# Softcap attention and two gated MLPs on one core: attention on four planner threads, first pairs by block rows, slots shared otherwise

## The chip, the core and the metric

The program runs on one core of a Trainium2 chip. A core has five engines with queues of their own: TensorE (matmuls and their weight loads), VectorE (DVE), ScalarE (ACT), GpSimd (POOL) and SyncE (SP), which here starts the DMAs. They run beside each other and wait for each other through semaphores. The metric is the device time of one execution in microseconds (us); lower is better.

## What is computed

Attention with softcapped scores for 4 batches and 12 heads of 448 tokens and 64 columns; its output, 1792 tokens by 768, goes through a gated MLP (768 to 1536 to 768, sigmoid gate) and then through a second one (768 to 2048 to 768) whose activation is h cos(h). The weights arrive as 64-bit floats.

```python
scores = scale * np.matmul(q, k.transpose(0, 1, 3, 2))
scores = cap * np.tanh(scores / cap)
scores = scores - np.max(scores, axis=-1, keepdims=True)
attn = np.exp(scores)
attn = attn / (np.sum(attn, axis=-1, keepdims=True) + 1e-09)
x = np.matmul(attn, v)           # then (batch, token, head * 64)
gate = 1.0 / (1.0 + np.exp(-(x @ w_gate)))
x = gate * (x @ w_val) @ w_out
h = x @ w_in
out = (h * np.cos(h)) @ w_out2
```

## The kernel before

**Arithmetic.** Every matmul operand is split into a high and a low part that TensorE takes at its fast rate, and a product is three matmuls: high by high, high by low, low by high (`mm3`, `mm3s`). The names in the trace follow this: `wh`, `wl` are a weight tile's parts, `xh`, `xl` or the two halves of `x` those of the activations, `gh`, `gl` those of the gated product, `zh`, `zl` those of the hidden layer of the second MLP. The high part is a cast on ScalarE, the low part a subtraction on VectorE or GpSimd (`high`, `low`, `block_split`). A weight is converted from 64-bit words first (`convert`: two operations on ScalarE, L420 and L421, four on VectorE, L424, L432, L440 and L448); the result is kept in DRAM for later use (`kept`). Weights of the second MLP are converted in the background (`bg`, tiles `bf`, `braw`).

**Stages.** The tokens go in two halves of 896 (two batches each). Attention runs over 24 pairs of heads, batch by batch; pair i has transposes of q and k (L1329, split into `qs` and `ks` on VectorE, L1336 and L1340), four score products (L1363), tanh (L1374) and exp (L1394) on ScalarE, sums on GpSimd (L1406) and VectorE (L1417, "softmax total"), the product with the values (L1434), the sum over partitions (L1453), a reciprocal (L1467) and a product with it. For the first 12 pairs the result is split into `xh` and `xl`, for the last 12 it is kept as `x1r`. Then follow, for the first half, the gate and value products (`gate_value_plain`, stage A of half 0: 24 tiles of 6 steps of 6 matmuls) and the output product (`result`, stage B). For the second half the gate and value products, and for both halves the first product of the second MLP, are made in pairs of weight tiles: `pair_products` makes seven products of half the size in place of eight (numbers 1 to 7, made in the order 1, 2, 6, 5, 7, 4, 3, each over three blocks j of the contraction, 63 matmuls in all). It takes sums of blocks of the activations (`block_sums`, tiles `x`, `t`, `yr`, `y`, `x1r`) and of the weights (`sums`), and `pair_sums` evicts the seven products from their banks (L816, L825). The whole order is: attention; A and B of half 0; A (first pair products) and B of half 1; the cosine stage of half 1, then of half 0, each with eight pair products C, whose results go through the chain `hidden` (u, n, u, sine, u = h times cosine, zh, zl), and four output groups D (`out_group`), in the order C C C D C C D C C C D D.

**What sets the order.** Nothing is ordered by hand. Generators ("threads") yield operations, and `Order.run` takes the operation that could start first by a table of durations, plus a penalty of its thread; the engines' queues then hold the operations in that order. Threads wait on conditions: a free slot of 49 half-size tiles (`mids`, `get`, `get_w` with a range of weight tiles per stage, W_A0 to W_CD), one of five big tiles (`bigs`), a bank of PSUM, or a word in `done`. Attention is one thread with penalty 0, so its operations enter the queues in the order in which they are written, on whatever engine they run. `whole`, which issues all other TensorE work, has penalty 4 us until attention ends, the weights' threads 0.3 (W_PEN). First weights are loaded from pair 18 on (W_FROM), and until attention ends three are converted at most (LEAD).

## Time and profile before

| | us |
|---|---|
| median of 3 runs | 1239.87 (1237.41 to 1241.43) |
| the profiled execution | 1238.03 |
| its span, first to last instruction | 1236.2 |
| TensorE busy (matmuls) | 1177.0 (95%) |
| VectorE busy | 929.1 (75%) |
| ScalarE busy | 672.1 (54%) |
| GpSimd busy | 252.4 (20%) |
| mean granted TensorE clock | 0.983 |

In the profile, PE is TensorE, DVE VectorE, ACT ScalarE, POOL GpSimd. L708 and L720 are the lines of all matmuls of the plain and of the pair products, L1226 that of the output groups. TensorE's matmuls overlap, so its busy time is a union; time per matmul is read from a long stretch without waits. A wait is the idle time of an engine before an instruction, with the instruction that ended it. By time: attention ends near 247 us, A and B of half 0 near 406 and 495, A and B of half 1 near 661 and 755; the cosine stage of half 1 ends near 999, that of half 0 at 1232.

### The profile page before, as it was taken

What the parts mean: (1) busy time and instruction counts of PE and PEld (TensorE: products, weight loads), DVE (VectorE), ACT (ScalarE), POOL (GpSimd) and SP (SyncE); (2) the same over time, 40 slices, a digit from 0 to 9 for tenths busy, and PEclk for the clock granted to TensorE, in tenths of its full rate; (3) what the DMA queues carried; (4) which work ended last, traced back from release to release, by engine and by line L of the source; (5) the groups of instructions that cost most, each with busy time, mean ns of one, the idle gap of its engine ahead of it and who ended that gap; (6) DMA issues with size and microseconds to landing.
All of it is one profiled execution on the core that took longest, in us unless ns stands there. A gap on an engine that the chain in (4) does not pass through costs nothing.

```text
span 1236.2 us, 15864 instructions
## 1 busy us (share of the span) xinstructions
PE 1177.0 (95%) x6090; PEld 995.7 (81%) x6090; DVE 929.1 (75%) x1128; ACT 672.1 (54%) x785; POOL 252.4 (20%) x139
## 2 busy tenths in 40 slices
PE   8999978999999999999998998889999998999998
PEld 4444545599999999888887996789999997989898
DVE  6999886689887966888889645865678878275862
ACT  6888876756555644444446433665347347361730
POOL 3666543400011000223321000111122212011200
PEclk9999998999999999999998998899999998999999
DMA  7432233177876575334433730112106322121203
GB/s 181 109 79 68 71 85 91 57 256 229 276 258 204 186 253 183 130 128 141 159 111 121 260 141 17 56 44 77 39 26 205 90 77 77 38 66 39 77 1 90
DMA packets 126187, 148.16 MB, mean 120 GB/s; under 512 B 49952, under 2 KB 98976, under 8 KB 126112
## 3 DMA queue, kind: packets, MB, share of 16 engines
q1 hardware_dynamic: 125824, 147.09, 38.4%
q8 instruction: 48, 0.79, 0.3%
q14 instruction: 27, 0.22, 0.1%
q10 hardware_dynamic: 288, 0.07, 0.0%
HBM read 112.13 MB, written 35.00 MB: 119 GB/s over the span
## 4 chain that ended last, share of the span: by engine, by line
PE 70%; DVE 7%; ACT 2%; issue 2%; DVEq 0%; ACTq 0%
PE pt L708 28%; PE pt L720 23%; PE pt L1226 18%; DVE wl L494 1%; DVE zl L1167 1%; ACT wh L483 1%; DVE h L816 1%; DVE val L816 1%; DVE x L1052 1%; DVE sg L893 1%; DVE e L648 1%; ACT x L1046 0%; PE pt L1434 0%; DVE part L816 0%; DVE u L1150 0%
## 5 line engine op out<-in xcount | busy, mean ns | idle before, releaser
L720 PE MATMUL pt<-x,wh 128*128 128x448 f32 x1260 | 349.4, 373 | 10.5 <-DVE x L1052 4.3
L720 PEld LDWEIGHTS pt<-x,wh 128*128 128x128 f32 x1260 | 239.1, 190 | 40.1 <-ACT x L1046 7.2
L494 POOL TENSOR_TENSOR wl<-f,wh 128x768 fp32r<-128x768 f32 x53 | 101.8, 1922 | 442.3 <-ACT wh L483 403.3
L720 PE MATMUL pt<-x,wl 128*128 128x448 f32 x504 | 188.3, 374 | 3.7 <-DVE wl L494 2.9
L483 ACT CAST wh<-f 128x768 fp32r<-128x768 f32 (+1 forms) x164 | 123.3, 777 | 83.6 <-DVE f L648 47.8
L1226 PE MATMUL pt<-wh,zh 128*128 128x384 f32 x448 | 151.1, 337 | 9.2 <-ACT zh L1164 9.2
L1226 PE MATMUL pt<-wh,zl 128*128 128x384 f32 x448 | 151.2, 337 | 4.4 <-DVE zl L1167 4.4
L1226 PE MATMUL pt<-wl,zh 128*128 128x384 f32 x448 | 150.4, 336 | 0.0
L1374 ACT ACTIVATE p<-pt,tanh_scale 112x896 f32<-112x896 f32 x96 | 92.0, 1009 | 46.1 <-PE pt L1363 46.1
L720 PEld LDWEIGHTS pt<-x,wl 128*128 128x128 f32 x504 | 95.9, 190 | 17.3 <-DVE wl L494 8.6
L494 DVE TENSOR_TENSOR wl<-f,wh 128x768 fp32r<-128x768 f32 x83 | 82.3, 996 | 21.2 <-ACT wh L483 20.9
L1249 DVE TENSOR_TENSOR acc<-pt,acc 128x384 f32<-128x384 f32 x84 | 46.7, 556 | 63.2 <-PE pt L1226 62.5
L1226 PEld LDWEIGHTS pt<-wh,zh 128*128 128x128 f32 x448 | 84.8, 189 | 10.6 <-ACT zh L1164 10.5
L1226 PEld LDWEIGHTS pt<-wh,zl 128*128 128x128 f32 x448 | 84.6, 189 | 6.5 <-DVE zl L1167 6.5
L708 PE MATMUL pt<-gl,wh 128*128 128x448 f32 x288 | 83.5, 372 | 3.7 <-DVE gl L937 3.7
L1434 PE MATMUL pt<-p,v 112*64 112x448 f32 x384 | 77.5, 545 | 9.6 <-ACT p L1374 9.6
L1394 ACT ACTIVATE p<-p,cap_sb 112x1792 f32<-112x1792 f32 x48 | 86.2, 1797 | 0.0
L708 PE MATMUL pt<-xh,wh 128*128 128x448 f32 x288 | 85.4, 378 | 0.0
L1363 PEld LDWEIGHTS pt<-qs,ks 64*112 64x112 f32 x576 | 47.0, 173 | 47.2 <-ACT p L1374 21.2
L1226 PEld LDWEIGHTS pt<-wl,zh 128*128 128x128 f32 x448 | 84.8, 189 | 0.1
L708 PE MATMUL pt<-xl,wh 128*128 128x448 f32 x288 | 84.5, 375 | 0.0
L708 PE MATMUL pt<-xh,wl 128*128 128x448 f32 x288 | 84.3, 374 | 0.0
(115 smaller groups left out, 2075.9 us busy)
## 6 DMA issues: line engine op xcount, KB each, us to landing
f<-kept SPq DMA_DIRECT2D x100, 384.0 KB, 3.4
kept<-f SPq DMA_DIRECT2D x36, 384.0 KB, 3.2
braw<-in_moe_w_in_dram SPq DMA_DIRECT2D x16, 768.0 KB, 6.7
kept<-bf SPq DMA_DIRECT2D x32, 384.0 KB, 2.8
braw<-in_moe_w_out_dram SPq DMA_DIRECT2D x16, 768.0 KB, 6.4
raw<-in_moe_w_gate_dram SPq DMA_DIRECT2D x12, 768.0 KB, 5.7
raw<-in_moe_w_val_dram SPq DMA_DIRECT2D x12, 768.0 KB, 5.2
raw<-in_moe_w_out_dram SPq DMA_DIRECT2D x12, 768.0 KB, 5.6
```

The costliest lines, as they stand in the source:

```text
L483: yield act(n, lambda: nc.scalar.copy(out=at(h, 0, n), in_=at(src, o, n)), sc, [h.cell("h")])
L494: lambda e: e.tensor_tensor(out=w.part(1, 0, n), in0=at(src, o, n), in1=w.part(0, 0, n).bitcast(F32), op=ALU.subtract),
L648: lambda: nc.vector.tensor_tensor(out=at(dst, d0, HW), in0=at(x, x0, HW), in1=at(y, y0, HW), op=op),
L708: nc.tensor.matmul(b.ap[:, c, s0:s1], lhsT=w.part(wi, kk * P, P), rhs=x.part(xi, c * S + s0, s1 - s0), start=(first and (wi, xi) == (0, 0) ...
L720: nc.tensor.matmul(b.ap[:, c, s0:s1], lhsT=w.part(wi, o, P), rhs=x[xi][:, s0:s1], start=(first and (wi, xi) == (0, 0)), stop=(last and (wi ...
L816: lambda: nc.vector.tensor_tensor(out=out, in0=src, in1=part, op=ALU.add),
L1226: nc.tensor.matmul(b.ap[:, 0, :NB], lhsT=at(z[zi], t * P, P), rhs=w.part(wi, k * NB, NB), start=(first and (zi, wi) == (0, 0)), stop=(last ...
L1249: lambda: nc.vector.tensor_tensor(out=o, in0=ps(b, 0, NB), in1=o, op=ALU.add),
L1363: nc.tensor.matmul(ps(b, h)[:CP], lhsT=at(ks, ki * S + c * CP, CP)[r], rhs=at(qs, qi * S, S)[r], start=(n_ == 0), stop=(n_ == 2),)
L1374: lambda: nc.scalar.activation(out=two(at(p, 2 * j * S, 2 * S))[:CP], in_=both(b)[:CP], func=AF.Tanh, scale=tanh_scale[:CP],),
L1394: lambda: nc.scalar.activation(out=pv, in_=pv, func=AF.Exp, scale=cap_sb[:CP]),
L1434: nc.tensor.matmul(ps(b)[h * D : (h + 1) * D], lhsT=tv[:CP, h, c, :], rhs=at(p, (2 * j + h) * S, S)[:CP], start=(c == 0), stop=(c == NC - 1),)
```

## The change

Attention becomes four threads, one for each of TensorE, ScalarE, GpSimd and VectorE (`on_pe`, `on_act`, `on_pool`, `on_dve`); what one makes for another is handed over in a dictionary, so each engine's attention work keeps its own order, and other work can be placed between on one engine without the others. The planner subtracts a tenth of the time that an operation has been ready from its penalty (AGE). `whole` has penalty 1 during attention instead of 4 (A_PEN), first weights are loaded from pair 12, and the limit of three converted ones is lifted. The first pair product of each stage that makes pairs goes block row by block row: for each j all seven products, instead of each product over all j (`by_rows`); seven banks are held until the end. `block_sums` finishes all seven blocks of one j before the next j. Slots: wider or shifted weight ranges in stage A of half 1 and in the last stages, two weight pairs loaded ahead instead of three (F_AHEAD), g tiles and the hidden chain's u and n may take a big slot, an attention tile p is freed by its last two readers, and the second half's pair weights are loaded from the last tile of B of half 0 on.

```diff
 class Order:
     LAT = 0.12
+    AGE = 0.1
...
-                pen = th.pen() if callable(th.pen) else th.pen
+                if th.since is None:
+                    th.since = t
+                pen = (th.pen() if callable(th.pen) else th.pen) - self.AGE * (t - th.since)
...
-    LEAD, AHEAD = 3, 4
+    F_AHEAD = 2
+    H_PEN, S_PEN = 0.4, 0.0
+    LEAD, AHEAD = 99, 4
...
-    W_PEN, W_FROM = 0.3, 18
+    W_PEN, W_FROM = 0.3, 12
+    ATT_PEN, A_PEN = 0.0, 1.0
...
-    W_A0, W_B0, W_A1, W_B1, W_CD = (7, 14), (7, 14), (9, 15), (8, 14), (10, 14)
+    W_A0, W_B0, W_A1, W_B1, W_CD = (7, 14), (7, 14), (14, 18), (8, 14), (12, 16)
...
-            yield lambda: len(loaded) < 3
+            yield lambda: len(loaded) < F_AHEAD
...
+        for js in [[j] for j in range(KH)] if by_rows else [range(KH)]:
+            for i in (1, 2, 6, 5, 7, 4, 3):
+                if js[0] == 0:
+                    if i in (1, 3):
+                        at_bank[i] = ((yield from bank()), 0)
...
+                yield from product(i, *at_bank[i], g, X, js, last_use)
+                if js[-1] == KH - 1:
+                    ready.add(i)
...
-                return hf == 1 and "converted" in done and ("B", 0) in done and bigs.left > 0
+                return hf == 1 and ("B", 0) in done and bigs.left > (0 if "converted" in done else BG_RAW)
...
-            yield from pair_products(("pair", "g", p), X, False, GateSink(p))
+            yield from pair_products(("pair", "g", p), X, False, GateSink(p), p == 0)
...
+            if n == KD - 1 and hf == 0:
+                done.add("again")
...
             yield from direct(j, 2)
-        for j in range(KH):
             yield from first_sums(j)
-            yield from later(j, 6)
-        for i in (5, 7, 4, 3):
-            for j in range(KH):
-                yield from direct(j, i) if i == 3 else later(j, i)
+            for i in (6, 5, 7, 4):
+                yield from later(j, i)
+            yield from direct(j, 3)
...
-        u, r = mids.alloc("u", F32), mids.alloc("n", F32)
+        zh = None
+        if in_big():
+            u = bigs.alloc("u", F32)
+            u.refs = 2
+            r, ro = u, n
+            zh = mids.alloc("zh", F32R)
+        else:
+            u, r, ro = mids.alloc("u", F32), mids.alloc("n", F32), 0
...
-            yield from pair_products(("pair", "i", i), X, last, HiddenSink(hf, i))
+            yield from pair_products(("pair", "i", i), X, last, HiddenSink(hf, i), i == 0)
...
+        for gen, name in ((on_pe, "PE"), (on_act, "ACT"), (on_pool, "POOL"), (on_dve, "DVE")):
+            spawn(gen(), ATT_PEN, f"attention {name}")
...
-        spawn(whole(), lambda: 0.0 if "att" in done else 4.0, "PE")
+        spawn(whole(), lambda: 0.0 if "att" in done else A_PEN, "PE")
```

The changed kernel's line numbers differ: L1395 is the score product, L1374 the transposes, L1420 the values product, L1441 the sum over partitions, L715 a plain step, L1575 and L1579 the split of q and k, L1614 the reciprocal, L1623 the product with it, L1593 the softmax total, L431, L439, L447 and L455 the conversion, L501 a weight's low part, L1065 and L1079 a block's low part and a block sum, L827 an eviction, L655 a weight sum, L904 value by gate, L948 gl.

On TensorE, the 17th pair of heads in the kernel before, one values product to the next:

```order
L1434 MATMUL pt<-p_1370,v_1305 64x448 x4
L1434 MATMUL pt<-p_1408,v_1305 64x448 x4
L1363 MATMUL pt<-qs_1316,ks_1348 112x448 x6
L1363 MATMUL pt<-qs_1388,ks_1420 112x448 x6
L1329 MATMUL pt<-ident,qk_1443 128x112 x4
L1453 MATMUL pt<-sum_1417,ones 64x448 x2
L1363 MATMUL pt<-qs_1388,ks_1420 112x448 x12
L1329 MATMUL pt<-ident,qk_1446 128x112 x4
```

And the first pair that holds steps in the changed kernel, pair 15:

```order
L1420 MATMUL pt<-p_1271,v_1156 64x448 x4
L1395 MATMUL pt<-qs_1196,ks_1249 112x448 x6
L715 MATMUL pt<-xh_422,wh_1294 128x448 x2
L715 MATMUL pt<-xl_423,wh_1294 128x448 x2
L715 MATMUL pt<-xh_422,wl_1324 128x448 x2
L1395 MATMUL pt<-qs_1262,ks_1331 112x448 x6
L1374 MATMUL pt<-ident,qk_1303 128x112 x4
L1441 MATMUL pt<-sum_1292,ones 64x448 x2
L1395 MATMUL pt<-qs_1262,ks_1331 112x448 x12
L715 MATMUL pt<-xh_503,wh_1294 128x448 x2
L715 MATMUL pt<-xl_504,wh_1294 128x448 x2
L715 MATMUL pt<-xh_503,wl_1324 128x448 x2
```

The plain steps now begin at pair 15, three of them ahead of its values product, where the kernel before begins with pair 18; ahead of the last values product stand 20 steps, before 16.

On VectorE, attention with the first weight conversion, in the kernel before:

```order
L1467 RECIPROCAL r_1544<-pt 128x448
L1480 TENSOR_TENSOR x1r_1546<-pt,r_1544 128x448
L424 TENSOR_SCALAR f_1517<-f_1517 128x768
L432 TENSOR_SCALAR f_1517<-f_1517 128x768
L440 SCALAR_TENSOR_TENSOR f_1517<-raw_1516,f_1517 128x768
L448 SCALAR_TENSOR_TENSOR f_1517<-f_1517,raw_1516 128x768
L1417 SCALAR_TENSOR_TENSOR sum_1489<-sum_1489,guard,p_1480 112x896
L1336 CAST ks_1580<-pt 128x448
L1340 TENSOR_TENSOR ks_1580<-pt,ks_1580 128x448
```

And a conversion in the changed kernel:

```order
L431 TENSOR_SCALAR f_1454<-f_1454 128x768
L439 TENSOR_SCALAR f_1454<-f_1454 128x768
L447 SCALAR_TENSOR_TENSOR f_1454<-raw_1453,f_1454 128x768
L1575 CAST qs_1577<-pt 128x448
L1579 TENSOR_TENSOR qs_1577<-pt,qs_1577 128x448
L1614 RECIPROCAL r_1614<-pt 128x448
L1623 TENSOR_TENSOR x1r_1615<-pt,r_1614 128x448
L455 SCALAR_TENSOR_TENSOR f_1454<-f_1454,raw_1453 128x768
L1593 SCALAR_TENSOR_TENSOR sum_1550<-sum_1550,guard,p_1541 112x896
L1575 CAST ks_1655<-pt 128x448
```

The conversion's four operations, in one piece ahead of the softmax total before, stand in two places of the pair now; the first conversion (pairs 11 to 14) stands in four.

On VectorE, the end of the second half's value products and the start of its output product, in the kernel before:

```order
L893 TENSOR_TENSOR sg_5188<-val_5310,sg_5188 128x896
L816 TENSOR_TENSOR val_5260<-pt,part_5215 128x448
L893 TENSOR_TENSOR sg_5138<-val_5260,sg_5138 128x896
L937 TENSOR_TENSOR gl_5217<-sg_4074,gh_5216 128x896
L937 TENSOR_TENSOR gl_5332<-sg_4120,gh_5331 128x896
L937 TENSOR_TENSOR gl_5342<-sg_4288,gh_5341 128x896
L937 TENSOR_TENSOR gl_5352<-sg_4333,gh_5351 128x896
```

And in the changed kernel, where two g tiles have been split above these rows:

```order
L827 TENSOR_TENSOR val_5248<-pt,part_5214 128x448
L904 TENSOR_TENSOR sg_5182<-val_5301,sg_5182 128x896
L904 TENSOR_TENSOR sg_5139<-val_5248,sg_5139 128x896
L501 TENSOR_TENSOR wl_5313<-f_5280,wh_5297 128x768
L439 TENSOR_SCALAR bf_5218<-bf_5218 128x768
L948 TENSOR_TENSOR gl_5273<-sg_4321,gh_5272 128x896
L447 SCALAR_TENSOR_TENSOR bf_5218<-braw_5005,bf_5218 128x768
L948 TENSOR_TENSOR gl_5338<-sg_4365,gh_5337 128x896
L455 SCALAR_TENSOR_TENSOR bf_5218<-bf_5218,braw_5005 128x768
L948 TENSOR_TENSOR gl_5349<-sg_4526,gh_5348 128x896
```

Before, all twelve gl stand in one run (one weight's low part among them); now a background conversion's operation stands between one gl and the next.

On VectorE, the start of the cosine stage, the blocks of j = 2 in the changed kernel (y_5904 and y_6026 are the last two output tiles):

```order
L1065 TENSOR_TENSOR x_6074<-t_6057,x_6074 128x448
L1065 TENSOR_TENSOR x_6082<-t_6057,x_6082 128x448
L1079 TENSOR_TENSOR y_5904<-y_6026,y_5904 128x448
L1079 TENSOR_TENSOR y_6026<-y_6026,t_6057 128x448
L655 TENSOR_TENSOR f_5760<-f_5760,e_6025 128x384
L1065 TENSOR_TENSOR x_6096<-y_5904,x_6096 128x448
L501 TENSOR_TENSOR wl_6109<-f_5808,wh_6107 128x768
L827 TENSOR_TENSOR h_6117<-pt,part_6100 128x896
L827 TENSOR_TENSOR part_6100<-pt,h_6117 128x896
L655 TENSOR_TENSOR e_6133<-f_5981 128x384
L1065 TENSOR_TENSOR x_6103<-y_6026,x_6103 128x448
L1065 TENSOR_TENSOR x_6135<-y_6026,x_6135 128x448
```

In the kernel before the blocks of all three j stand in this place, product by product, and of the evictions only the first stands among them; now the blocks of j = 0 and 1 stand higher up, and the last two of j = 2 (products 4 and 3) stand behind the first two evictions of the same pair product.

## Rows read from the trace of the kernel before

**Rows 1.** stages of the span; columns are length, then each engine's busy time, clock, DMA

```profile
163.00:243.20 80.20, 70.25 (x368) 41.95 (x368) 57.00 (x48) 56.82 (x51) 33.23 (x16) 0.91 0.32 87
...
243.20:405.90 162.70, 162.70 (x790) 145.57 (x790) 136.03 (x166) 93.58 (x108) 11.55 (x6) 1.00 0.74 242
...
495.20:660.60 165.40, 159.76 (x758) 140.56 (x757) 140.95 (x178) 80.54 (x109) 45.21 (x24) 1.00 0.42 137
...
660.60:754.90 94.30, 90.58 (x434) 83.42 (x433) 56.93 (x73) 36.58 (x45) 0.00 (x0) 0.96 0.46 155
...
754.90:811.30 56.40, 47.82 (x191) 39.13 (x190) 47.61 (x61) 34.99 (x49) 10.00 (x6) 0.88 0.16 50
...
811.30:844.20 32.90, 29.72 (x170) 29.08 (x169) 14.46 (x17) 16.20 (x25) 0.64 (x1) 1.00 0.06 15
...
1038.20:1075.60 37.40, 31.63 (x170) 30.80 (x169) 15.30 (x18) 17.02 (x26) 0.00 (x0) 0.91 0.05 14
```

**Rows 2.** what TensorE waited for over the span: total, times, longest

```profile
PE pt L1434 <- ACT p L1374: 9.6, 13, 2.4
...
PE pt L1226 <- ACT zh L1164: 9.2, 4, 5.4
...
PE pt L1226 <- DVE zl L1167: 4.4, 6, 1.7
...
PE pt L720 <- DVE x L1052: 4.3, 7, 2.8
...
PE pt L708 <- DVE gl L937: 3.7, 1, 3.7
```

**Rows 3.** TensorE's timeline, values products of five pairs: start, length, what they are

```profile
111.49 3.23 PE L1434 MATMUL pt<-p,v 112*64 112x448 f32 x16 [0.59 <-ACT p L1374]
...
144.56 3.23 PE L1434 MATMUL pt<-p,v 112*64 112x448 f32 x16
...
152.50 3.23 PE L1434 MATMUL pt<-p,v 112*64 112x448 f32 x16
...
162.90 3.23 PE L1434 MATMUL pt<-p,v 112*64 112x448 f32 x16 [2.40 <-ACT p L1374]
...
243.16 2.10 PE L1434 MATMUL pt<-p,v 112*64 112x448 f32 x10
```

**Rows 4.** same view as rows 1, of a head pair each

```profile
111.49:120.09 8.60, 8.01 (x52) 3.99 (x52) 8.19 (x9) 7.06 (x7) 5.34 (x4) 1.00 0.32 79
144.56:152.50 7.94, 7.94 (x54) 4.00 (x53) 6.97 (x8) 7.06 (x7) 4.21 (x3) 1.00 0.31 99
162.90:179.83 16.93, 12.60 (x64) 7.29 (x65) 16.48 (x15) 12.39 (x11) 7.71 (x4) 0.90 0.41 110
```

**Rows 5.** VectorE's softmax totals, min/median/max ns; its conversion operations, busy and mean ns

```profile
L1417 DVE SCALAR_TENSOR_TENSOR sum<-sum,guard,p x24: 1140/1142/4787, 21.1 to 240.2; 112x896 f32<-112x896 f32 x24
...
L440 DVE SCALAR_TENSOR_TENSOR f<-raw,f 128x768 int32<-128x768 int32 x36 | 34.5, 957 | 1.1
...
L432 DVE TENSOR_SCALAR f<-f 128x768 int32<-128x768 int32 x36 | 21.8, 606 | 1.2
```

**Rows 6.** VectorE's gl group, 661 to 684: times, busy and mean ns

```profile
L937 DVE TENSOR_TENSOR gl<-sg,gh 128x896 fp32r<-128x896 f32 x12 | 12.2, 1083 | 0.0
```

**Rows 7.** the start of the cosine stage: a window before it, two VectorE groups, ScalarE

```profile
720.00:755.00 35.00, 35.00 (x175) 32.43 (x174) 10.26 (x16) 7.36 (x11) 0.00 (x0) 1.00 0.15 50
...
L816 DVE TENSOR_TENSOR h<-pt,part 128x896 f32<-128x896 f32 x6 | 6.5, 1091 | 2.2 <-PE pt L720 2.1
...
L1052 DVE TENSOR_TENSOR x<-t,x 128x448 fp32r<-128x448 f32 x5 | 3.0, 620 | 0.7 <-ACT x L1046 0.6
...
754.97 0.91 ACT L1026 COPY y<-pt 128x896 f32<-128x896 f32 x1 [11.73 <-PE pt L708]
```

**Rows 8.** the second output group's start, 1036 to 1052: TensorE, then VectorE

```profile
1044.71 0.69 PE L1226 MATMUL pt<-wh,zh 128*128 128x384 f32 x1 [5.41 <-ACT zh L1164]
...
1041.93 2.09 DVE L1161 TENSOR_TENSOR u<-h,u 128x896 f32<-128x896 f32 x2
```

393 lines of the change are left out of this document (228 added, 165 removed).

## Prediction

> **What bounds the kernel now.** I read the stages first, then who waits on TensorE, then the two engines it waits for. The stages [rows 1]: between 243.2 and 405.9 us TensorE is busy for all 162.7 us, 790 matmuls at 0.206 us each. That is the price of a matmul at full clock, and every stage is held against it: 6 matmuls (one step of a gate or value tile) are 1.24 us, 63 (one pair product) 13.0, 21 (one block row of a pair product) 4.3, 3 (one block of one product) 0.62. A page of the profile puts TensorE at 95% busy, so what can be won is its waits and the stretches at the lower of its two clock levels (1.2 of 2.4 GHz). By stage [rows 1]:
>
> - Attention's end, 163 to 243.2: 70.25 us busy of 80.2, mean clock 0.91.
> - First pair products, 495.2 to 660.6: 756 matmuls should take 155.7 us and take 165.4; 9.7 lost.
> - The second half's first output, 660.6 to 754.9: 432 matmuls, 89.0 against 94.3; 5.3 lost, clock 0.96.
> - The first three cosine pairs, 754.9 to 811.3: 189 matmuls, 38.9 against 56.4; 17.5 lost, clock 0.88.
> - First output group of either half (811.3 and 1038.2): 32.9 and 37.4 us for the same 168 matmuls.
>
> Who is waited for [rows 2]: ScalarE's exp in attention (9.6 us), the zh and zl of the output groups (9.2 and 4.4), the split blocks x (4.3 from VectorE alone) and the first gl (3.7, one wait). [...] So the sum goes stage by stage: which wait goes, and what is late next.
>
> **Attention's second half.** A quiet pair of heads takes 7.94 us, and TensorE is busy for all of it (VectorE 6.97, ScalarE 7.06); while the first half's x is also split, the pair takes 8.60 and VectorE (8.19) is the slowest [rows 4]. In the order, pairs 0 to 10 stand on all engines as before, so they cost the same. From pair 12 on (values product at 111.49) to the last one at 243.16 the kernel before takes 131.7 us [rows 3]. TensorE's own work in it is 12 x 7.94 + 16 steps x 1.24 - 1.6 (the last pairs transpose nothing) = 113.5: 18.2 lost. Where: quiet pairs lose nothing (144.56 to 152.50), the first pair with a weight conversion 2.5 (152.50 to 162.90), the next 16.93 - 10.4 = 6.5, with VectorE 16.48 of 16.93 busy [rows 3, 4]. A conversion's four operations (0.6, 0.6, 0.96 and about 1 us [rows 5]) stand there in one piece between reciprocal and softmax total, and the total, the cast of ks and the next scores stand behind them.
>
> After, 20 steps stand before the last values product, conversions begin at pair 11, and of their four operations one to three stand in a place. Per pair that is 10.4 to 11.7 us on TensorE from pair 15 on, against about 6.97 + 2.2 = 9.2 on VectorE. Where no step stands yet (11 to 14) the conversion's 1.0 to 1.2 us show: VectorE 9.2 to 9.4 where the pair took 8.6; that costs some 2 us. Further waits I put at 7.5 us, 0.8 a pair from 15 on: the pieces are half as long as before, and the steps lie between. So 9.5 lost instead of 18.2: **-8.7**. Bounds: 3 (the pairs without a step alone), which is -15, and 22 (every pair with a piece loses 2.5, as the first did), which is +4. The four steps brought forward are counted by the difference in loss; after attention nothing waits before 495 us [rows 1], so a step earlier is a step saved there.
>
> **First pair products.** The background conversions on VectorE fall from 41 operations to 22 in this stage (counted in the orders), and up to three more weight slots may be held (14 to 18, was 9 to 15), so the waits for weights should fall from 9.7 us to about 2.7. But the first pair now goes block by block. Its last block row starts 8.6 us into the stage; its fourth and third products need blocks that VectorE makes behind two evictions, which themselves wait for products of that same row: by the order the second eviction (5 and 7 done at 11.7, 1.09 each [rows 7]) ends at 12.9 and six operations of 0.5 to 1 us follow to the last block, 16.8. TensorE waits 4 us. Together **-3.0** (-7 to +3; half of either term).
>
> **Second half's first output.** A big slot may now take a g tile before the conversions are done; two of twelve g tiles are split early. But from the third on, conversion operations stand between the gl (the order below). From TensorE's end of the pair products: eviction 0.7, two products with sg to 2.8, a weight's wl 3.7 (768 columns, 0.96 [rows 5]), conversion 4.3, third gl 5.3, and then one gl per 1.02 us [rows 6] plus 0.6 to 0.96 of conversion, to the twelfth at 21.2. Twelve steps alone would end at 14.8; with the last gl they end near 22: 7.2 lost where 5.3 were: **+1.9** (-2 to +4).
>
> **The cosine stage.** Before, block sums go product by product over all three j, so most blocks wait for the last output tile; VectorE does most of them behind it, while from 720 to 755 it was busy for 10.26 us of 35 [rows 7]. After, j = 0 and j = 1 are finished in that idle time and TensorE has two block rows, 8.6 us, before it needs j = 2. ScalarE's copy of the last tile ends at 0.9 [rows 7]; the first three blocks of j = 2 are ready at 3.4, 4.0 and 6.8 (0.62 us an operation [rows 7]), the block of product 7 at 9.0, all before their turn. Products 4 and 3 again stand behind two evictions and one more operation: 12.9 + 0.6 + 0.6 = 14.1 against a turn at 11.7, 2.2 us of waiting. The pair ends at 15.2, the third at 41.2. What is late next is the hidden chain of the second pair: its product u on VectorE stands behind the third pair's evictions (39.4), so the two zl of the first output step come at 46.3 and 47.3, about 4.5 us late. Before, the stage lost 17.5 and the group start 2.9 (the 32.9 us against 30.0, which is 168 at the rate of its undisturbed part); after, 2.2 + 4.5: **-13.7** (-9 to -17).
>
> **Second half of it.** Its blocks were ready in time before, so block rows win nothing and put the first pair's evictions up to 1.7 us later. At its first output group TensorE waited 5.41 us for zh, with u and zl following it on VectorE [rows 8], and the 37.4 us at clock 0.91 hold another 3.4 of the lower clock [rows 1]; by the same reckoning as above the wait is now about 4.1. **-2.5** (-6 to 0). The other group starts: about 1 us less for two of them, **-0.8** (-3 to +1).
>
> **At nothing.** Earlier loads of the pair weights ("again" one tile sooner): the stage's DMA share is at most 0.74 [rows 1]. Seven banks held by a first pair: the eighth takes the next pair's first product, and the two-bank eviction is out 3.1 us after the last row began, before the second asks. Aging in the planner works through the orders counted above. For what I did not count, the 250 us from 243 to 495 that lose nothing now and can only lose, I add **+2** (0 to +4).
>
> Sum: -8.7 - 3.0 + 1.9 - 13.7 - 2.5 - 0.8 + 2 = -24.8. The profiled execution took 1238.03 us (1236.2 span and 1.8 around it), so 1213.2; the median of the runs shown is 1.84 above it: **1215 us**.
>
> **Rivals.**
> 1. The cosine start wins, attention does not. VectorE is already at 6.97 of 7.94 in a quiet pair [rows 4], and a softmax total took up to 4.79 us instead of 1.14 [rows 5]. If the loss in attention stays at 18 and the block rows in the first pair products cost what they save, 11.7 is missing: 1227. Against: steps stand where VectorE was waited for.
> 2. Everything fits better. The waits I walked are taken in turn, with no overlap; of the 34 us I left as waits (9.5, 6.7, 7.2, 6.7, 4.1), a third gone gives 1204, half 1198.
> 3. Slower: VectorE held up by GpSimd. In a pair of heads GpSimd is busy 4.21 us of 7.94 [rows 4] with sums from SBUF, and the conversion pieces now stand in the same pairs. The long total lost 4.79 - 1.14 = 3.65 us [rows 5]. VectorE has 98 us of work in pairs 12 to 23 (the order's operations by the durations above) against the 128 I allow; with 1.3 such holds in every one of twelve pairs it needs 155 and nothing is won; with 1.6 it needs 168, and the kernel takes 1255. Against: one total of 24 is that long before [rows 5], with three conversions in the stretch. The Trainium skill bears on this: "SBUF — State Buffer", section "SBUF: two separate sides", has the second port pair as an exclusive lock, held for a whole instruction, between GpSimd and a VectorE operation with two SBUF inputs; the last two operations of a conversion are of that kind. The longest total agrees with such a lock, its median of 1142 ns shows that it is rarely met; by the rule alone each piece would wait for half of GpSimd's 4.21 us per 7.94, some 0.55 us on average, inside my 0.8.
> 4. It does not do what it says. Attention held 16 steps before and holds 20 now, so little is interleaved that was not; if only that moved, 1235.
>
> **How the numbers follow.** Chances: forecast (1206 to 1224) 0.54; rival 1 (1224 to 1232) 0.18; rival 2 (below 1206) 0.18; rival 4 and other mixtures between 1232 and 1244 0.06; rival 3 0.04. The range reaches from rival 2's end to rival 1's upper side, 1198 to 1232, and leaves out the slower cases and a fifth of rival 2. About 0.3% (3.7 us) is what a measurement of this kernel tells from no change. Faster 0.91, same 0.04, slower 0.05.
>
> **What would show it.** In the profile after: values products 12 to 23 apart by 10 to 12 us and the last near 234 to 240; two to four long waits for x at the first pair of the stages near 485 and 745, each under 3 us; gl waits of 0.3 to 0.8 us in a row behind the pair products; three cosine pairs in about 41 us where 56.4 stood; first output groups waiting 4 to 5 us for zl. It is wrong if attention's end does not move, if totals or conversions on VectorE are often over 2 us, or if weights (wh, wl) are waited for at the block rows.

## The result, and the profile after

The changed kernel takes **1195.54 us** in the median (1195.09 to 1199.94, 4 runs) where the kernel before takes 1239.12 (1237.41 to 1241.43, 4 runs, on the same chip): ratio 0.9655, 95% interval 0.9627 to 0.9683. Forecast were 1215 us and a range of 1198 to 1232. The sign was right; the time lies 2.5 us below the range and the gain is 43.6 us where 24 were forecast.

Stretches of the changed kernel, in the columns of [rows 1] (length; TensorE, its weight loads, VectorE, ScalarE, GpSimd busy; clock; DMA):

```profile
108.91:232.12 123.21, 118.76 (x703) 65.46 (x702) 111.73 (x101) 103.50 (x92) 63.43 (x31) 1.00 0.35 93
...
387.40:475.00 87.60, 87.60 (x434) 81.19 (x433) 69.58 (x99) 47.35 (x61) 1.79 (x1) 1.00 0.67 225
474.90:638.40 163.50, 158.52 (x758) 143.44 (x757) 127.49 (x167) 72.17 (x100) 36.22 (x20) 0.98 0.36 119
638.40:732.70 94.30, 90.19 (x434) 80.34 (x433) 71.41 (x100) 44.69 (x58) 0.00 (x0) 1.00 0.49 163
732.70:773.50 40.80, 38.65 (x191) 35.41 (x190) 31.76 (x40) 28.96 (x39) 12.69 (x7) 1.00 0.28 88
773.50:808.80 35.30, 31.22 (x170) 30.58 (x169) 14.62 (x18) 16.87 (x27) 0.00 (x0) 0.95 0.04 12
1000.90:1036.90 36.00, 32.33 (x170) 31.50 (x169) 14.70 (x18) 16.94 (x27) 0.00 (x0) 0.91 0.04 12
```

The first line is attention from the values product that stands at 111.49 in [rows 3] to the last one. The three cosine pairs take 40.8 us where [rows 1] has 56.4. What TensorE still waits for (total, times, longest), against [rows 2]:

```profile
PE pt L1255 <- ACT zh L1193: 6.1, 2, 3.1
PE pt L1420 <- ACT p L1486: 4.2, 7, 0.6
PE pt L715 <- DVE gl L948: 4.1, 6, 2.2
PE pt L727 <- DVE x L1065: 3.7, 2, 2.2
PE pt L727 <- ACT x L1059: 3.4, 1, 3.4
```

Stage by stage, from the end of TensorE's last matmul of one stage to that of the next in its timeline (us):

| stage | before | changed | difference | forecast |
|---|---|---|---|---|
| attention to the values product of [rows 3], first row | 111.49 | 108.91 | -2.6 | 0 |
| from there to the last values product | 131.7 | 123.2 | -8.5, and 4 steps more inside: -13.4 | -8.7 |
| rest of the first half's gate and value tiles, those 4 steps counted here | 162.9 | 160.3 | -2.6 | +2 (with the next) |
| first half's output | 89.3 | 87.6 | -1.7 | |
| first pair products | 165.4 | 163.4 | -2.0 | -3.0 |
| second half's first output | 94.2 | 94.3 | +0.1 | +1.9 |
| three cosine pairs and first output group | 89.3 | 76.1 | -13.2 | -13.7 |
| second half of the cosine stage, first output group | 37.45 | 35.9 | -1.6 | -2.5 |
| the four other output groups | 181.1 | 176.0 | -5.2 | -0.8 |
| sum | | | -42.2 | -24.8 |

The sum is the difference of the spans, 1236.2 and 1194.0. So 17.4 us were missed, in four places: attention (4.7 and 2.6), TensorE's own pace behind it (6.3), the other output groups (4.4). The rest is within 2 us each.

### The profile page after: what moved, and what is told of

Same layout as the page of the kernel before. It is cut to its first block, busy times and chain, and to the rows that moved or that the text cites. A ratio compares the mean times of both kernels' runs of the same rounds, so it can differ in the third digit from the quotient of the medians.

```text
span 1194.0 us, 15877 instructions
## 1 busy us (share of the span) xinstructions
PE 1159.2 (97%) x6090; PEld 989.7 (83%) x6090; DVE 913.1 (76%) x1127; ACT 668.6 (56%) x785; POOL 258.6 (22%) x140
## 4 chain that ended last, share of the span: by engine, by line
PE 88%; DVE 7%; ACT 2%; issue 1%; SPq 0%; DMA 0%; DVEq 0%; ACTq 0%
PE pt L727 30%; PE pt L715 28%; PE pt L1255 19%; PE pt L1420 5%; PE pt L1395 4%; DVE r L1614 1%; ACT p L1486 1%; PE pt L1374 1%; PE pt L1441 1%; ACT p L1503 1%; DVE sum L1593 1%; DVE gl L948 1%; DVE zl L1196 1%; DVE h L827 0%; SPq L1329 0%
## 5 line engine op out<-in xcount | busy, mean ns | idle before, releaser
L727 PE MATMUL pt<-x,wh 128*128 128x448 f32 x1260 | 344.6, 369 | 7.1 <-DVE x L1065 3.7
L727 PE MATMUL pt<-x,wl 128*128 128x448 f32 x504 | 185.7, 368 | 0.0
L501 POOL TENSOR_TENSOR wl<-f,wh 128x768 fp32r<-128x768 f32 x41 | 80.1, 1957 | 381.8 <-ACT wh L490 297.3
L501 DVE TENSOR_TENSOR wl<-f,wh 128x768 fp32r<-128x768 f32 x95 | 96.8, 1024 | 45.9 <-ACT wh L490 45.6
L715 PE MATMUL pt<-gl,wh 128*128 128x448 f32 x276 | 79.4, 369 | 4.1 <-DVE gl L948 4.1
L715 PE MATMUL pt<-xh,wh 128*128 128x448 f32 x288 | 83.4, 371 | 0.0
L715 PE MATMUL pt<-xl,wh 128*128 128x448 f32 x288 | 81.8, 365 | 0.0
L715 PE MATMUL pt<-xh,wl 128*128 128x448 f32 x288 | 81.8, 365 | 0.0
L1420 PE MATMUL pt<-p,v 112*64 112x448 f32 x384 | 77.5, 545 | 4.2 <-ACT p L1486 4.2
L1395 PEld LDWEIGHTS pt<-qs,ks 64*112 64x112 f32 x576 | 46.2, 171 | 41.9 <-ACT p L1486 16.7
```

The lines of the kernel that those rows point to most:

```text
L501: lambda e: e.tensor_tensor(out=w.part(1, 0, n), in0=at(src, o, n), in1=w.part(0, 0, n).bitcast(F32), op=ALU.subtract),
L715: nc.tensor.matmul(b.ap[:, c, s0:s1], lhsT=w.part(wi, kk * P, P), rhs=x.part(xi, c * S + s0, s1 - s0), start=(first and (wi, xi) == (0, 0) ...
L727: nc.tensor.matmul(b.ap[:, c, s0:s1], lhsT=w.part(wi, o, P), rhs=x[xi][:, s0:s1], start=(first and (wi, xi) == (0, 0)), stop=(last and (wi ...
L1395: nc.tensor.matmul(ps(b, h)[:CP], lhsT=at(ks, ki * S + c * CP, CP)[r], rhs=at(qs, qi * S, S)[r], start=(n_ == 0), stop=(n_ == 2),)
L1420: nc.tensor.matmul(ps(b)[h * D : (h + 1) * D], lhsT=tv[:CP, h, c, :], rhs=at(p, (2 * j + h) * S, S)[:CP], start=(c == 0), stop=(c == NC - 1),)
```

## The experiments

Each kernel was timed beside the kernel before on its own chip, where that one's median was 1238.2 to 1242.3; a ratio is the time over that median. Times from different chips are compared with that spread of some 4 us in mind.

**The same kernel twice.** No edit.

> The kernel before, unchanged, profiled a second time. In the first profile TensorE's matmuls of 448 columns follow each other at 206.7 ns in the 248 us after attention, and in the changed kernel at 202.7 ns: 1200 matmuls, 4.8 us. Theory: which of the two a stretch runs at is settled at the last stall ahead of it and can differ from one execution of the same kernel to the next; this profile then shows 202.7 in at least one long stretch that had 206.7, and the time lies between 1233 and 1242. Rival: it belongs to the kernel's own order of instructions; every stretch then has the same figure as in the first profile. Pairs 1 to 12 of attention (8.60 us each in the first profile, 7.94 in four of them after) answer the same question for that difference of 2.6 us.

1240.3 us. The stretch behind attention has 206.7 ns again, and the pairs of attention take 8.60 as in the first profile. But the second half's first output, at 202.7 ns in the first profile, is at 206.7 in this one. The last two cosine pairs ahead of the first output group go the same way, and the first pair products, a mixture of both figures in the first profile, are nearly all at 202.7 here. So part of the theory holds (one kernel, two figures in one stretch), and for the two differences it was made for it does not.

> The changed kernel, unchanged, profiled a second time. In the first profile its 448-column matmuls follow at 202.7 ns from 240 to 486 us, at 206.7 from 496 to 640, at 202.7 from 660 to 770. Theory: the stretch behind attention keeps its figure in every execution of a kernel (in both profiles of before it had 206.7, in all others so far 202.7), the stretches behind a later wait may change. Rival: any stretch may change, and the 4.7 us between this kernel's fastest and slowest time are one stretch at the other figure.

1195.9 us. Two stretches of the changed kernel in its first profile, then in its second (columns as above; no wait in any of them, clock 1.00):

```profile
500.00:630.00 130.00, 130.00 (x631) 118.08 (x630) 101.14 (x134) 53.07 (x73) 27.90 (x16) 1.00 0.32 106
660.00:740.00 80.00, 80.00 (x396) 74.15 (x396) 54.74 (x84) 37.92 (x52) 0.00 (x0) 1.00 0.49 163
```

```profile
250.00:387.40 137.40, 137.40 (x680) 127.32 (x679) 117.79 (x146) 82.01 (x96) 9.05 (x5) 1.00 0.75 247
500.00:630.00 130.00, 130.00 (x644) 120.48 (x643) 103.39 (x136) 55.03 (x75) 27.91 (x16) 1.00 0.34 112
660.00:740.00 80.00, 80.00 (x389) 72.67 (x388) 54.52 (x84) 36.51 (x52) 0.00 (x0) 1.00 0.47 158
```

The same matmuls in the same order: 631 and then 644 in 130 us (206 and 202 ns each), 396 and then 389 in 80 us. The two stretches changed places, and the span is the same within 0.1 us. The stretch behind attention kept its figure in both.

**Attention alone.** The four threads, the aging, the weights from pair 12 on (W_FROM), lead 99, penalty 1.0 put into the kernel before.

> The kernel before with the attention part alone: the four engine threads, the aging of waiting threads, the early start of the weights and the low penalty of the plain steps. Theory: attention is worth what the two traces show up to its last values product, 13.5 us from pair 12 on and up to 2.6 before, and up to 4.4 more if TensorE's quicker cadence follows it: 1219 to 1226, with 18 to 22 steps ahead of the last values product. Rival, my forecast's size: 8.7, so 1230. Rival, interplay: it is worth little without the rest: above 1233.

1221.2 us (1219.5 to 1222.3), ratio 0.985 (0.982 to 0.988), as the theory has it. The first half's gate and value tiles end at 388.6, as in the changed kernel (387.4). But the first pair products take 169.9 (165.4 before), the second half's first output 97.2 (94.2): 7.5 us are given back there. The four other output groups have the changed kernel's lengths.

**All but attention.** The attention of before in the changed kernel, with its constants.

> The changed kernel with the attention of before: its one thread, weights from pair 18 on, penalty 4.0, three units of lead; the block rows, the block order, the shared slots stay, and so does the aging. Theory: the parts add, so 1195.5 + 16 = 1211.5, and up to 1216 if the slower cadence comes with it; the cosine stage keeps its 20 us. Rival, interplay: under 1205 or over 1220.

1218.0 us (1216.8 to 1219.9), between the theory and its rival. The gains of this run and of the run before it, 22.6 and 19.4 us against the kernel before on the same chip, make 42.0 of the changed kernel's 43.6: they add in sum, but not stage by stage. (The aging is in both runs.) The first half's output, 87.6 us in the changed kernel, takes 98.9: TensorE waits 4.9 us for one wl there, 8.3 in all, and loses clock.

**Attention's threads alone.** The changed kernel with the constants of before:

```diff
-    LEAD, AHEAD = 99, 4
+    LEAD, AHEAD = 3, 4
-    W_PEN, W_FROM = 0.3, 12
-    ATT_PEN, A_PEN = 0.0, 1.0
+    W_PEN, W_FROM = 0.3, 18
+    ATT_PEN, A_PEN = 0.0, 4.0
```

> The changed kernel's four attention threads with the constants of before: weights from pair 18, lead 3, penalty 4.0. Against the run with the attention of before, the threads are the one difference; there the end of the first half's gate and value tiles came at 398.8 us and the output after it took 98.9. Theory: the threads by themselves are the gain: end of the gate and value tiles at 385 to 389, in all 1194 to 1200. Rival: it needs the constants (steps let in by the low penalty, lead): 394 to 400 and 1210 to 1218.

1191.6 us (1189.0 to 1194.1), ratio 0.9616 (0.958 to 0.965): not distinguishable from the changed kernel, and 26 us below the run with the attention of before, from which it differs in the threads alone. The gate and value tiles end at 390.5 (398.8 there); this profile has 206.7 ns behind attention, which is 3 us of it (679 matmuls in 140 us, 680 in 137.4 in the changed kernel). First this kernel, from its values product at 109.47 to its last one, then the one with the attention of before, the same stretch:

```profile
109.47:211.10 101.63, 96.25 (x600) 47.78 (x600) 87.86 (x85) 87.92 (x76) 59.68 (x29) 0.98 0.28 70
```

```profile
111.45:239.81 128.36, 116.68 (x685) 64.76 (x685) 99.96 (x93) 98.69 (x87) 60.48 (x30) 0.97 0.29 77
```

With 3 steps inside, the first has 93.7 + 3.7 us of work by the reckoning of the prediction and loses 4.2; the second has 17 steps, 114.8, and loses 13.6. So up to the end of the gate and value tiles the threads are worth 8.3 of the 26 us. The other 17.5 come later: 6.7 in the first half's output (92.2 us against 98.9) and 10.8 in the first pair products, where this run does not wait at all, with the same block rows (first this run, then the one with the attention of before):

```profile
482.60:636.00 153.40, 153.40 (x758) 141.92 (x757) 126.00 (x160) 72.10 (x99) 41.33 (x24) 1.00 0.38 127
```

```profile
497.70:661.90 164.20, 158.96 (x757) 143.91 (x756) 124.98 (x165) 73.39 (x101) 35.53 (x20) 0.98 0.35 114
```

That the threads are the cause is shown by the two runs. How the order that they leave behind spares these later stages is not.

**The early start taken back.** Weights from pair 18 on (W_FROM 18), all else as changed; then the same with the one thread of before.

> The changed kernel, but weights may be loaded and converted only from pair 18 of attention on, as before, and not from 12. Theory: the gain in attention is VectorE's conversions spread over more pairs, so that most of the 13.5 us goes: 1204 to 1209, with pairs of 14 to 17 us again. Rival: it is the finer order of the four threads, and the early start adds little: 1196 to 1200, with about 16 steps ahead of the last values product.

1196.8 us (1193.2 to 1197.7): the rival by its time. Only 5 steps, not 16, stand before the last values product, which comes at 212.7; the first half's output then waits 3.6 us once, for a gl, and the first pair products take 158.75 instead of 163.4.

> The changed kernel with attention again one thread, and weights from pair 18; lead 99, penalty 1.0 and aging as in the changed kernel. Against the run that had only the weights from pair 18 on, the four threads are the one difference. Theory: the threads are the gain, since one thread lays a conversion's operations between two of attention's: 14 to 18 us lost again from pair 12 on, 1206 to 1212. Rival: the lead, the lower penalty and the aging are the gain: 1195 to 1200, pairs of 8 to 11 us.

1217.1 us (1214.3 to 1219.6), ratio 0.980, some 20 us above the run with four threads. The sign is the theory's, the size is above its range, and the manner is another: with one thread and the low penalty 48 steps are put between attention's, pairs last 12 to 22 us, and TensorE waits 8.1 us for one wh behind them.

**The aging alone, and all without it.** In the kernel before:

```diff
...
+    AGE = 0.1
...
-                pen = th.pen() if callable(th.pen) else th.pen
+                if th.since is None:
+                    th.since = t
+                pen = (th.pen() if callable(th.pen) else th.pen) - self.AGE * (t - th.since)
...
```

> The kernel before with the aging alone: a waiting thread's penalty falls by 0.1 per microsecond that it waits. The kernel with the attention part alone already shows output groups of 29.7, 58.2, 29.7 and 58.2 us where the kernel before has 31.0, 58.8, 31.0 and 60.3; it has neither the shared slots nor the new weight ranges. Theory: the 5.2 us there, and 1.5 at the second half's first group, are the aging's alone: the same four lengths here, and 1230 to 1235 in all. Rival: they come from the order that attention leaves behind: lengths as in the kernel before, 1238 to 1243.

1242.2 us (1238.2 to 1245.0), ratio 1.000 (0.998 to 1.002): the lengths of the theory, the sum of the rival. An output group, then the first pair products and the second half's first output:

```profile
883.90:913.60 29.70, 29.38 (x170) 29.06 (x169) 17.00 (x26) 8.16 (x10) 1.85 (x1) 1.00 0.10 28
495.40:666.20 170.80, 160.37 (x758) 141.80 (x758) 144.17 (x193) 83.94 (x114) 43.36 (x23) 0.99 0.46 153
666.20:766.70 100.50, 92.95 (x434) 81.71 (x433) 41.69 (x53) 27.51 (x35) 0.00 (x0) 0.98 0.26 87
```

The group takes 29.7 us where the kernel before needs 31.0, and the two others 170.8 and 100.5 where it needs 165.4 and 94.3 [rows 1]. Aging alone is a trade.

> The changed kernel with aging at 0. In the kernel before, aging alone moved nothing in sum: 6.7 us better in the cosine stage, and as much worse at the first pair products, the first output of the second half and the first cosine pairs. Theory: in the changed kernel the block order takes away that loss, so aging is worth its 5 to 7 us: 1200 to 1204, output groups of 31.0, 58.8, 31.0, 60.3 again. Rival: still a trade, 1193 to 1199.

1210.3 us (1204.0 to 1213.0), ratio 0.977, above the theory's range. The changed kernel without aging is 14 us slower: no plain step at all is put into attention, the gate and value tiles end 8.3 us later and the first half's output takes 5.8 more; the six output groups take 14.1 us more, 7.4 of them in the four other groups (30.7, 63.7, 30.7 and 58.25 us, not the lengths of the kernel before). The first pair products (156.2) and the output behind them (89.3) are 12 us shorter than with it.

**The order of the block sums.** A product's three blocks together, as before:

```diff
-            yield from first_sums(j)
-            for i in (6, 5, 7, 4):
-                yield from later(j, i)
-            yield from direct(j, 3)
+        for j in range(KH):
+            yield from first_sums(j)
+            yield from later(j, 6)
+        for i in (5, 7, 4, 3):
+            for j in range(KH):
+                yield from direct(j, i) if i == 3 else later(j, i)
```

> The changed kernel with the block sums in the order of before (a product's three blocks together), the first pairs by block rows. Theory: the block order carries the cosine start, since most blocks of j = 0 and 1 again come after the last output tile: 10 to 17 us lost there, 1204 to 1211. Rival: the rows alone do it, each row asks for a block only every 0.6 us: 1196 to 1200.

1217.2 us (1212.0 to 1219.2), ratio 0.980 (0.975 to 0.984): the theory's loss at the cosine start, and more in all than its range. The three cosine pairs take 55.1 us again, as in the kernel before (56.4), the first pair products 168.3 (163.4 in the changed kernel):

```profile
474.90:643.20 168.30, 160.36 (x758) 143.60 (x757) 132.96 (x178) 78.56 (x109) 37.11 (x22) 0.97 0.39 130
739.00:794.10 55.10, 45.78 (x191) 38.27 (x190) 41.85 (x59) 33.44 (x48) 10.98 (x5) 0.85 0.19 58
```

**The block rows.** All first pairs product by product, as before (by_rows is False everywhere).

> The changed kernel with all seven products of a first pair one after the other, as before. Theory: block rows and block order are both needed: at the cosine start the first product reaches j = 2 after 2.5 us and waits for blocks that come at 3.4 to 9, so some 6 to 8 us of waiting return there, while the 8.4 us at the first pair products (4.98 of waiting and half of 6.8) go; in sum 1194 to 1200. Rival: the rows carry the cosine start's 13 us: 1203 to 1209. Rival: the block order alone carries it and the rows cost: under 1192.

1185.4 us (1182.8 to 1189.5), ratio 0.955 (0.952 to 0.959): the third theory, and some 10 us better than the changed kernel. The first pair products, the three cosine pairs, the first output group, and the second half's first output group:

```profile
474.80:635.80 161.00, 158.39 (x757) 142.85 (x756) 125.56 (x167) 72.75 (x100) 35.68 (x20) 0.99 0.36 121
730.10:771.00 40.90, 39.40 (x190) 35.26 (x190) 32.89 (x41) 29.37 (x39) 12.20 (x7) 1.00 0.23 68
771.00:804.30 33.30, 31.18 (x170) 30.52 (x169) 12.82 (x16) 16.15 (x26) 0.00 (x0) 0.95 0.04 12
996.40:1026.90 30.50, 29.63 (x170) 29.01 (x169) 13.40 (x16) 17.02 (x27) 0.00 (x0) 1.00 0.05 14
```

They take 2.5 us less, the same, 2 less and 5.5 less than with the rows.

**The shared slots.** Hidden tiles in mid slots only, g tiles in big slots only after the conversions, 10 to 14 weight slots.

> The changed kernel with the slots as before: u and n of the hidden tiles in mid slots only, g tiles in big slots only after the last background conversion, 10 to 14 weight slots in the cosine stage. Theory: the shared slots carry little, 1193 to 1200, since the output groups have the same lengths in a kernel without them. Rival: they are what lets the hidden tiles of the second pair be made in time: 1201 to 1210, with 3 us or more of waiting at each group's start.

1195.4 us (1192.5 to 1200.6), ratio 0.967 (0.961 to 0.972): the theory. They carry nothing that can be measured. No run takes back the wider weight range of the second half's gate and value stage, the two pairs loaded ahead or the earlier loads by themselves, so what each of these is worth is not known.

**Versions meant to beat both.** All are without block rows.

> No block rows, and weights from pair 18 of attention on. Early start and late start gave the same time with the rows (1195.5 and 1196.8): what attention lost less came back as waiting in the first half's output (3.7 us and its clock) and 4.6 us less at the first pair products. Theory: the same trade without rows, 1183 to 1188. Rival: the first pair products' gain stays and the rest goes: 1178 to 1181.

1193.9 us (1192.6 to 1195.5): above either expectation. The early start is worth some 9 us here, though nothing with the rows; 3.6 us of waiting in the first half's output come back, and the first pair products, 158.75 with the rows, take 163.0. This is the other half of the answer on the rows. With the late start they save time in that stage (first with, then without):

```profile
480.40:639.20 158.80, 156.84 (x758) 141.72 (x757) 123.67 (x164) 73.72 (x102) 38.90 (x23) 1.00 0.36 123
```

```profile
479.20:642.10 162.90, 156.39 (x757) 142.96 (x756) 132.90 (x170) 75.67 (x104) 39.29 (x22) 0.99 0.38 127
```

TensorE waits 1.1 us for blocks there with the rows and 6.5 without. The three cosine pairs take 38.3 us with them and 40.9 without; the two first output groups take 5.1 and 5.9 more with them. In sum the two kernels cannot be told apart (ratios 0.965 and 0.964).

> A version meant to beat both: no block rows, and three penalties lowered to -1.5 where TensorE waits: the block sums from the end of the output ahead of them, the second half's g tiles from the end of the pair products, the hidden tiles everywhere. Theory: the last waits of the run without rows (5.3 us lost at the first pair products, 5.0 at the second half's first output, 3.5 at the first output group) are VectorE doing other work first: a half to two thirds of 13.8 goes, 1176 to 1180. Rival: work put first only pushes evictions and weight conversions back, which TensorE then waits for: 1183 to 1190.

1192.3 us (1189.9 to 1194.9): the rival in its manner, above its range, though two of the gains are there. The first pair products take 153.2 us and the output behind them 90.1, and then TensorE stands still for a weight (all its waits of the kernel, the longest two):

```profile
PE pt L1256 <- DVE wl L501: 9.9, 1, 9.9
PE pt L1421 <- ACT p L1487: 4.2, 7, 0.6
```

> No block rows, and two of the three lowered penalties: block sums and the second half's g tiles first, the hidden tiles as in the changed kernel. With all three, the first pair products took 153.2 us (161.0 without any) and the second half's first output 90.1 (94.3), but the first output group 41.1 (33.2) and the two later third pairs 43.8 (39.05), waiting for weights. Theory: the gains of the first two and the losses of the third are independent: 1185.4 - 7.8 - 4.2 = 1173, range 1171 to 1177. Rival: the pushed-back weight conversions come from the first two: 1182 to 1190, with 8 to 10 us of waiting for wl at the first output group again.

1179.4 us (1177.4 to 1184.2), ratio 0.951 (0.947 to 0.955): the two gains whole, no wait for wl, but 38.1 us for the first output group (33.2 without the priorities), whose zh is 4.2 us late; the profile is of its slowest execution, 1184.2 us. Between the two expectations; 12.9 us of the loss of the run before it were the hidden tiles' priority, the one difference.

```diff
-        spawn(block_sums(X1, x1, lambda: x_room(0)), 0.8, "x1")
+        spawn(block_sums(X1, x1, lambda: x_room(0)), lambda: -1.5 if ("B", 0) in done else 0.8, "x1")
...
-        spawn(block_sums(Y1, y_raw[1], lambda: x_room(1)), 0.5, "y1")
+        spawn(block_sums(Y1, y_raw[1], lambda: x_room(1)), lambda: -1.5 if ("B", 1) in done else 0.5, "y1")
...
-            spawn(g_split(hf), 1.0, f"g{hf}")
+            spawn(g_split(hf), (lambda: -1.5 if ("A", 1) in done else 1.0) if hf else 1.0, f"g{hf}")
```

> As the run with the two lowered penalties, and the hidden tiles' penalty at 0.0 instead of 0.4, not at -1.5. Theory: a small step lets the hidden chain of a first output group pass one eviction (a zl some 1 us earlier) without pushing the third pair's weights back: 1 to 3 us less than the run with two. Rival: the same order nearly everywhere, no difference over 1 us.

1179.3 us (1177.6 to 1179.4), ratio 0.951 (0.948 to 0.954), the rival by its time. The order is not the same: the first output group takes 34.35 and the second half's 29.1, but two later groups 2.1 to 2.5 more each, for a wl. This version beats the changed kernel by 16 us. Its first pair products and the output behind them:

```profile
475.00:628.20 153.20, 153.20 (x758) 142.00 (x757) 131.04 (x163) 72.41 (x99) 40.72 (x24) 1.00 0.36 122
628.20:718.40 90.20, 89.64 (x434) 81.01 (x433) 69.08 (x97) 43.98 (x57) 0.00 (x0) 1.00 0.53 179
```

## Why the forecast fell short, by its own steps

Four terms of the sum failed. Attention's "further waits", put at 7.5 us, were not there (-8.7 forecast, -13.4 found). The first twelve pairs, put at nothing, gained 2.6. The +2 for the stretch behind attention was -4.3. The other output groups, at -0.8, gained 5.2.

**Attention: the right cause, too small a size.** The term was "Further waits I put at 7.5 us, 0.8 a pair from 15 on" and some 2 us before. Of the first row of the profile after, 4.45 us are TensorE's waits, at clock 1.00. They lie where the 2 us were: three pairs from 108.91 to 137.71 take 28.8 where three quiet ones are 23.8. From there nothing is lost. The timeline (start, length):

```profile
137.71 3.23 PE L1420 MATMUL pt<-p,v 112*64 112x448 f32 x16
...
232.12 1.35 PE L1420 MATMUL pt<-p,v 112*64 112x448 f32 x6
```

Nine pairs with their 20 steps in 94.4 us; 9 x 7.94 + 20 x 1.24 - 1.6 is 94.7. The same stretch in the kernel before:

```profile
111.49:243.16 131.67, 118.12 (x679) 66.02 (x679) 103.08 (x95) 101.06 (x89) 62.02 (x31) 0.95 0.28 75
```

TensorE was idle for 13.55 us of it and is for 4.45 now; the rest of the 13.5 us gained, some 4.4, goes with the clock, which was 0.95 and is 1.00. The four threads do most of that by themselves: the loss falls from 13.6 to 4.2 between the run with the attention of before and the one with the threads alone. VectorE shows how. Its groups in that stretch before the change, with the idle time ahead of them at the end:

```profile
L1467 DVE RECIPROCAL r<-pt 128x448 f32<-128x448 f32 x13 | 38.3, 2948 | 10.4 <-PE pt L1453 9.3 <-issue 1.1
L1417 DVE SCALAR_TENSOR_TENSOR sum<-sum,guard,p 112x896 f32<-112x896 f32 x13 | 21.8, 1680 | 2.2 <-POOL sum L1406 2.2
...
L1336 DVE CAST qs<-pt 128x448 fp32r<-128x448 f32 x9 | 5.6, 623 | 11.0 <-PE pt L1329 11.0
```

and after it:

```profile
L1614 DVE RECIPROCAL r<-pt 128x448 f32<-128x448 f32 x13 | 38.3, 2950 | 8.4 <-PE pt L1441 8.4
L1593 DVE SCALAR_TENSOR_TENSOR sum<-sum,guard,p 112x896 f32<-112x896 f32 x12 | 18.8, 1563 | 0.7 <-POOL sum L1531 0.7
L447 DVE SCALAR_TENSOR_TENSOR f<-raw,f 128x768 int32<-128x768 int32 x5 | 8.5, 1698 | 0.1
...
L1575 DVE CAST qs<-pt 128x448 fp32r<-128x448 f32 x9 | 5.5, 616 | 1.0 <-PE pt L1374 1.0
```

Before, the casts of qs waited 11.0 us on VectorE for TensorE's transposes while TensorE waited for what VectorE and ScalarE make: each stood behind the other in one common order. After, 1.0; the reciprocals' wait, 9.3 and 8.4, hardly moved. In the two runs that differ in the threads alone the casts (qs and ks) waited 14.5 us with one thread and 4.1 with four. I had charged the conversions' place; it was the common order.

**The first twelve pairs: a step left out.** That pairs 0 to 10 stand "on all engines as before, so they cost the same" was wrong by 2.6 us. The orders agree in operations and tiles, not in the banks of PSUM (the memory that TensorE writes to), which the rows I compared do not name. [rows 2] pointed there: the 9.6 us in 13 waits for "ACT p L1374" are for the tanh, which reads the banks of the scores, and not for the exp as the prediction read it. The same values product in both, with what it waits for (before, then after):

```
70 L1434 MATMUL pt<-p_338,v_279 64x448 [waits DMAHW0_49,Activation_49]
71 L1434 MATMUL pt<-p_338,v_279 64x448 x3
72 L1434 MATMUL pt<-p_375,v_279 64x448 x4
```

```
70 L1420 MATMUL pt<-p_351,v_272 64x448 [waits DMAHW0_49,DVE_49]
71 L1420 MATMUL pt<-p_351,v_272 64x448 x3
72 L1420 MATMUL pt<-p_383,v_272 64x448 [waits Activation_49]
```

Its first matmul took over a bank that ScalarE had read last, and now one that VectorE had; in the changed kernel's order that is so for pairs 1 to 4 and 11 (counted from 0), the five of the first twelve whose values product comes 7.94 us behind the one before. Three more of the first pairs are 7.94 us instead of 8.60 in every run with four threads and in none with one, and a fourth in all but one of those with the early start.

**Between attention and the pair products: wrong sign.** "The 250 us from 243 to 495 that lose nothing now and can only lose": +2 forecast, -4.3 measured. There is no wait in either; the matmuls came faster, 202.7 against 206.7 ns. I had taken 0.206 us for the price of a matmul. Nothing in the profile of before said that of this stretch; the second half's first output did, 432 matmuls of which most were at 202.7. This is no merit of the change that I can show: the run with the threads alone has 206.7 there, the kernel before with the aging alone 202.7. So 4.3 of the 43.6 us stay unexplained.

**First pair products: the sum by luck.** The waits for weights went altogether (2.7 forecast; the 9.7 that I called so were 5.6 us of idle time by [rows 1]), and the block row cost twice my 4 us: 3.44 and 1.54 of waiting, and 6.8 us at the lower clock behind the first, 3.4 more. The clock was the term I left out, though [rows 1] show it lower in most stages with such waits. VectorE in that wait (start, length, what it waited for):

```profile
486.63 1.09 DVE L827 TENSOR_TENSOR part<-pt,sg 128x896 f32<-128x896 f32 x1
487.64 0.55 DVE L655 TENSOR_TENSOR f<-f,e 128x384 f32<-128x384 f32 x1
488.10 0.62 DVE L1079 TENSOR_TENSOR x1r<-x1r,t 128x448 f32<-128x448 f32 x1
...
488.64 0.95 DVE L447 SCALAR_TENSOR_TENSOR bf<-braw,bf 128x768 int32<-128x768 int32 x1
...
489.54 2.18 POOL L501 TENSOR_TENSOR wl<-f,wh 128x768 fp32r<-128x768 f32 x1 [2.22 <-ACT wh L490]
489.98 2.77 DVE L1065 TENSOR_TENSOR x<-x1r,x 128x448 fp32r<-128x448 f32 x2
...
492.26 0.74 PE L727 MATMUL pt<-x,wh 128*128 128x448 f32 x1 [1.54 <-DVE x L1065]
```

The last two blocks stand behind an eviction, weight work and a conversion, as walked. Put first (the runs with lowered penalties, which have no block rows), they let TensorE run 153.2 us without a wait. But the block row does not wait of itself: with the threads alone the stage takes 153.4 us too, with the late start 158.75. The two blocks take 2.77 us, where such a pair takes 1.15 elsewhere in this trace, while GpSimd works on SBUF beside them; the port lock of the Trainium skill ("SBUF — State Buffer", section "SBUF: two separate sides") would do that, and the trace shows the coincidence, not the lock. The conversions in attention come nearer to it. One of them, started while GpSimd was at a sum:

```profile
120.11 2.11 POOL L1531 TENSOR_TENSOR sum<-p 112x896 f32<-112x896 f32 x1 [1.26 <-ACT p L1503]
120.19 2.85 DVE L447 SCALAR_TENSOR_TENSOR f<-raw,f 128x768 int32<-128x768 int32 x1
```

It ends 0.82 us behind GpSimd's operation, and an undisturbed one takes 0.96 in all; two other operations of a conversion that started so (at 171.67 and 185.94) end 0.84 and 0.82 behind GpSimd's. Of rival 3 this is what is true: in attention the L447 operations took 1698 ns on average, 957 in [rows 5]; but the totals took 1563, less than the 1680 of the same stretch before, and TensorE hardly noticed.

**Second half's first output: right in kind.** Waits for gl in a row, 2.16 and then 0.39 each, 4.1 in all; 7.2 forecast. With the g tiles put first it takes 90.1.

**Cosine start: right.** 2.2 us of waiting for blocks forecast, 2.15 found, by the chain that was walked; 4.5 at the first output group, 4.1 and 1.7 of clock found. (The group's length without waits is 29.1 us, 168 times 173.3 ns, and not the 30.0 that I took.) The block order does this: without it the stage is back at 55.1. That "block rows win nothing" in the second half was half of the truth: they cost 5.4 us there. That the first pair's later evictions do this is argued, not shown. In the changed kernel they win nothing anywhere; with the late start they saved some 4 us at the first pair products and 2.6 at the cosine pairs, and the groups behind took it back.

**The other output groups: -0.8 forecast, -5.2 found.** I took the aging for something that "works through the orders counted above". It is the cause: put into the kernel before by itself, it gives these lengths. But it is no gain by itself, since it lengthens the first pair products and the output behind them by 11.7 us; in the changed kernel the other edits take most of that away, and there it is worth 14 us. I did not find out which operations it moves at the group starts.

Of the rivals, the second ("everything fits better", a third to half of the waits gone, chance 0.18) came nearest; the time is below its 1198 too. For attention it is right. For the other four terms that it names, 24.7 us of waits were forecast and 19.0 found, and the clock, which I did not count after the change, cost 8.5 at three of them. These errors nearly cancel: the four stages gained 16.7 us where 17.3 were forecast, and that is luck. The rest of the miss is in terms that the rival does not name: the banks, the pace of the matmuls and the aging.

## What to carry to other kernels

Where one thread of a planner writes the work of several engines in one order, look for engines that wait for each other in turn (VectorE's casts 14.5 us for TensorE here); a thread for each engine, with no other constant changed, cut this to 4.1, and the gain went on into stages behind. Make the operands of the first product of a stage in the order in which the work behind the last late input becomes smallest, and put them ahead of evictions and conversions only for that stretch: that order was worth some 20 us (22 by the times, 18 by the ratios), and the priorities took 12 us out of two stages, of which 6 are left in the whole; a priority that lasts (the hidden tiles' at -1.5) cost 13, with TensorE waiting for weights. Take an edit back in more than one version before you call it good or bad: the block rows cost 10 us with the early start and nothing measurable with the late one. When two orders are compared, compare what each instruction waits for, not only its name.
